# Token transposes by DMA instead of TensorE in a fused cross-attention and maxout kernel

## The chip, the cores and the metric

The kernel runs on one core of a Trainium2 chip. A core has a matrix engine (TensorE, PE in the profile; its weight loads are the row PEld), a vector engine (VectorE, DVE), a scalar engine (ScalarE, ACT), a general engine (GpSimd, POOL) and a sync engine (SyncE, SP) that only issues DMAs. Each engine works off its own queue in order and waits on semaphores for the others. Sixteen DMA engines move the data for all queues. The metric is device time in microseconds for one execution; lower is better.

## The reference

There are 8 batches and 8 heads, each with 512 tokens and 32 state rows of 64 numbers. In every head the tokens read from the state and the state reads from the tokens; then a feed-forward layer with three first matrices, joined by a maximum, follows.

```python
# x: (8, 8, 512, 64), state: (8, 8, 32, 64), float32
scores  = scale * x @ state^T                # tokens look at the state rows
xread   = softmax(scores) @ state            # 512 rows per head
scores2 = scale * state @ x^T                # state rows look at the tokens
sread   = softmax(scores2) @ x               # 32 rows per head
z = concat([xread, sread], axis=2)           # (8, 8, 544, 64)
z = z.transpose(0, 2, 1, 3).reshape(8 * 544, 512)
h = max(z @ w1, z @ w2, z @ w3)              # d_ff = 768
out = h @ w_out                              # (4352, 512), float32
```

## The kernel before

**Layout.** For each batch `x_sb[b]` holds the tokens in bf16 as 128 partitions x 8 heads x 4 x 64: partition p has tokens 4p to 4p+3 of each head. Scores need the 64 numbers of a token on the partitions, so `xt_piece` (L124) makes `xT[b]`: 16 TensorE transposes of 128x128 (two token groups j at a time, 8 heads), all into one PSUM tile `pxt`, which ScalarE copies to SBUF in two halves (L134, L135; in batch 0 VectorE takes the second half). `xT` has two buffers.

**Attention of one batch.** `score_piece` (L137) multiplies `xT` with `bd`, the transposed state blocks, in 16 matmuls into the PSUM tile `ps`; ScalarE takes the exponential into `e` (L146), VectorE the sums `den` (L148) and their reciprocals `rden` (L150), and GpSimd the product `a` (L153; VectorE in batch 0). `e` serves both reads: `sread_piece` (L158) makes the state's read `psr`, which VectorE normalizes into `ats` (L176, L177); `at_piece` (L182) transposes `a` on TensorE into `pat`, which VectorE copies to `aT` (L190).

**Feed-forward.** The state is multiplied into the first matrices beforehand: `g_piece(b, u)` (L195), for u = 0 to 5, makes a sixth of `G[b]` = state x (w1 | w2 | w3), with the PSUM tile `pg` copied by ScalarE (L208). So `x_maxout(b, m)` (L229, with the work in `maxout`, L211) needs only `G` and `aT`: for each of the six column blocks m it fills three PSUM tiles `pw` with two matmuls each (L218), ScalarE copies the first (L222), and VectorE takes the maximum with the second (L223) and the third (L224) into `ht`. `ffn_out(b, j0, j1)` (L239) multiplies two groups of 128 rows of `ht` with `w_out` into `po` in 12 matmuls (L243), ScalarE copies it to `osb` (L251, three buffers), and SyncE stores it (L258).

**Buffers.** PSUM has four buffers of the tag `pw` and two of the tag `two`; `pxt`, `ps`, `psr`, `pat`, `pg` and `po` all take turns in these two. A new tile of the tag waits until the one before it in the same buffer has been copied out.

**Order.** The order of the instructions on every engine is the order of the program: the kernel sets a manual schedule. The main loop over b has six slots m, one after each `x_maxout(b, m)`. In the slots of batch b stands the attention of batch b + 1: `xt_piece` in slot 0, `score_piece` in slot 1, `sread_piece` in slot 3, `at_piece` in slot 4, and `g_piece(b + 1, u)` at the end of each slot u. The output of batch b - 1 stands at the head of slot 2 (first half) and of slot 5 (second half). In the last batch the slots hold the first layer for the state rows (`s_maxout`, L233) in place of the attention.

**Loads.** SyncE loads the tokens of batch 0 in float32. GpSimd's queue converts to bf16 as it loads: six loads of the first matrices, x(1), `w_out`, and from the loop x(b + 2) at the head of batch b (L275). GpSimd also computes `a`, so a load that stands behind an `a` in its queue is issued after it.

Of the kernel before, what the change touches and what calls it, by code (L numbers as in the profile page):

```python
# [15 lines left out]
def kernel(  # L16
# [14 lines left out]
    nc = tc.nc  # L31

    B, H, S, D = x.shape
# [25 lines left out]
    def x_rows(b):  # L59
        return x[b].rearrange("h (p j) d -> p h (j d)", j=J)  # L60

    x_sb = [data.tile([128, H, J, D], BF16, name=f"x{b}") for b in range(B)]
    st_f = data.tile([128, 16, D], F32, name="stf")
    nc.scalar.dma_start(
        out=st_f, in_=state.rearrange("b h n d -> (b h n) d").rearrange("(p t) d -> p t d", t=16))
# [7 lines left out]
    def load_x(b):  # L73
        nc.gpsimd.dma_start(out=x_sb[b].rearrange("p h j d -> p h (j d)"), in_=x_rows(b))
# [4 lines left out]
    def load_w(c):  # L79
        for i, w in enumerate((moe_w1, moe_w2, moe_w3)):  # L80
            nc.gpsimd.dma_start(
                out=w_sb[c][:, :, i * 384:(i + 1) * 384],
                in_=w.rearrange("(kk p) f -> p kk f", p=128)[:, :, c * 384:(c + 1) * 384],
            )

    load_w(0)
    load_w(1)
    load_x(1)
    nc.gpsimd.dma_start(out=wout_sb, in_=moe_w_out.rearrange("(kk p) f -> p kk f", p=128))

    ones = const.tile([128, 64], BF16, name="ones")
# [30 lines left out]
    xT, e, a, aT, G, ht = {}, {}, {}, {}, {}, {}  # L122

    def xt_piece(b):  # L124

        xT[b] = work.tile([128, H, 2, 128], BF16, tag="xT", name="xT")
        pxt = pp.tile([128, H, 2, 128], BF16, tag="two", name="pxt")
        for h in range(H):
            for jj in range(2):
                nc.tensor.transpose(  # L130
                    pxt[:, h, jj, :],
                    x_sb[b][:, h, 2 * jj:2 * jj + 2, :].rearrange("p j d -> p (j d)"), ident)
        second = nc.vector.tensor_copy if b == 0 else nc.scalar.copy
        nc.scalar.copy(out=xT[b][:, 0:4], in_=pxt[:, 0:4])  # L134
        second(out=xT[b][:, 4:8], in_=pxt[:, 4:8])  # L135

    def score_piece(b):  # L137
        ps = pp.tile([128, J, H, Ns], F32, tag="two", name="ps")
        for jj in range(2):
            for h in range(H):  # L140
                nc.tensor.matmul(  # L141
                    ps[:, 2 * jj:2 * jj + 2, slot(h), :], xT[b][:, h, jj, :],
                    bd[:, b, h].rearrange("p c n -> p (c n)"),
                    start=(h == 0), stop=(h == H - 1), skip_group_check=True)
        e[b] = work.tile([128, J, H, Ns], BF16, tag="e", name="e")
        nc.scalar.activation(out=e[b], in_=ps, func=AF.Exp, scale=scale)  # L146
        den = work.tile([128, J, H], F32, tag="den", name="den")
        nc.vector.reduce_sum(out=den, in_=e[b], axis=AX.X)  # L148
        rden = work.tile([128, J, H], F32, tag="rden", name="rden")
        nc.vector.reciprocal(out=rden, in_=den)  # L150
        a[b] = work.tile([128, J, H, Ns], BF16, tag="a", name="a")
        mul = nc.vector.tensor_mul if b == 0 else nc.gpsimd.tensor_mul
        mul(  # L153
            out=a[b].rearrange("p j h n -> p (j h) n"),
            in0=e[b].rearrange("p j h n -> p (j h) n"),
            in1=rden.rearrange("p j h -> p (j h)").unsqueeze(2).to_broadcast((128, J * H, Ns)))
# [38 lines left out]
    def g_piece(b, u):  # L195
        if u == 0:
            G[b] = work.tile([128, 2, 2 * HALF], BF16, tag="G", name="G")
        c, k = divmod(u, 3)
        pg = pp.tile([128, 2, 512], F32, tag="two", name="pg")
        for hh in range(NHP):  # L200
            for r in range(2):
                h = 2 * hh + r
                nc.tensor.matmul(  # L203
                    pg[32 * hh:32 * hh + 32, r, 0:384],
                    bd[64 * r:64 * r + 64, b, h, r, :],
                    w_sb[c][64 * r:64 * r + 64, hh, k * 384:(k + 1) * 384],
                    start=True, stop=True, tile_position=(64 * r, 32 * hh))
        nc.scalar.copy(out=G[b][:, :, u * 384:(u + 1) * 384], in_=pg[:, :, 0:384])  # L208
# [20 lines left out]
    def x_maxout(b, m):  # L229
        maxout(b, m, 512, lambda i, m, k: G[b][:, k, col(i, m):col(i, m) + 128],  # L230
               lambda k: aT[b][:, k, :], 2)

    def s_maxout(m):  # L233
        maxout("s", m, B * Ns,
               lambda i, m, k: w_sb[m // 3][:, k, col(i, m) % HALF:col(i, m) % HALF + 128],
               lambda k: ats[:, k, :], NHP)


    def ffn_out(b, j0, j1):  # L239
        po = pp.tile([128, 2, d_model], F32, tag="two", name="po")  # L240
        for j in range(j0, j1):
            for m in range(NM):
                nc.tensor.matmul(po[:, j - j0, :], ht[b][:, m, j * 128:(j + 1) * 128], wout_sb[:, m, :],  # L243
                                 start=(m == 0), stop=(m == NM - 1))
        n = j1 - j0
        o = work.tile([128, 2, d_model], F32, tag="osb", bufs=3, name="osb")
        if n == 1:
            nc.scalar.copy(out=o[:, 0, 0:256], in_=po[:, 0, 0:256])
            nc.vector.tensor_copy(out=o[:, 0, 256:512], in_=po[:, 0, 256:512])
        else:  # L250
            nc.scalar.copy(out=o, in_=po)  # L251
        if b == "s":
            for k in range(B):
                r0 = k * SP + S
                (nc.sync if k < 4 else nc.gpsimd).dma_start(
                    out=out[r0:r0 + Ns, :], in_=o[32 * (k % 4):32 * (k % 4) + 32, k // 4, :])
            return
        nc.sync.dma_start(  # L258
            out=out[b * SP:b * SP + S, :].rearrange("(p j) f -> p j f", j=J)[:, j0:j1, :],
            in_=o[:, 0:n, :])  # L260


    xt_piece(0)
    score_piece(0)
    bd_piece(1, B)
# [4 lines left out]
    for u in range(3, NG):  # L270
        g_piece(0, u)

    for b in range(B):
        if b + 2 < B:
            load_x(b + 2)  # L275
        slots = [[] for _ in range(NM)]
        if b + 1 < B:
            for f, m in ((xt_piece, 0), (score_piece, 1), (sread_piece, 3), (at_piece, 4)):
                slots[m].append(lambda f=f: f(b + 1))
            for u in range(NG):  # L280
                slots[u].append(lambda u=u: g_piece(b + 1, u))
        else:
            for m in range(NM):
                slots[m].append(lambda m=m: s_maxout(m))
        if b > 0:
            slots[2].insert(0, lambda: ffn_out(b - 1, 0, 2))
            slots[5].insert(0, lambda: ffn_out(b - 1, 2, 4))
        for m in range(NM):
            x_maxout(b, m)
            for f in slots[m]:  # L290
                f()
# [34 lines left out]
```

## Time and profile before

| what | before |
|---|---|
| median of three executions (lowest, highest), us | 190.43 (189.60, 203.50) |
| profiled execution, us | 189.44 |
| its span, first to last instruction, us | 187.6 |
| TensorE busy, us (share of the span) | 163.5 (87%) |
| ScalarE busy | 106.2 (57%) |
| VectorE busy | 103.3 (55%) |
| GpSimd busy | 28.0 (15%) |
| mean granted TensorE clock | 0.996 |
| period of one batch in the steady state, us | 19.04 |

A line of groups gives the source line, the engine, the operation, what it writes and reads, the number of instructions, their busy time with the mean of one in ns, and the idle time of the engine ahead of them with what ended it. A line of the timeline gives the start in us, the duration in us, the engine, the line and the operation, and in square brackets how long the engine was idle before it and what released it. In the rows of tenths, each digit is the busy share of one of 40 slices of the span, 4.7 us each. A DMA line ends with the median time in us from the issue to the landing of the data.

### The profile page before, as it was taken

Reading aid. Unit: us, or ns where it says so; the run is one execution under the profiler, and the core shown is the slowest. Engines: PE = TensorE matmul, PEld = TensorE weight load, DVE = VectorE, ACT = ScalarE, POOL = GpSimd, SP = SyncE. Lnnn points to the kernel's source line nnn. Section 1 sums busy time; section 2 is a strip of 40 time slices with the busy share of each in tenths; the row PEclk is TensorE's granted clock in tenths of the full one; section 3 lists DMA queues with packets and bytes.
Section 4 is the critical chain, followed back from the end, with each engine's and each line's share of the span. In section 5 each row is a group of like instructions: output and inputs, shape, how many; then the busy total and the mean of one; then the engine's idle time right before and its main releaser. Section 6 shows DMA issues by size and latency. Waiting matters only on the chain.

```text
span 187.6 us, 3845 instructions
## 1 busy us (share of the span) xinstructions
PE 163.5 (87%) x1604; PEld 84.8 (45%) x1604; DVE 103.3 (55%) x161; ACT 106.2 (57%) x151; POOL 28.0 (15%) x31
## 2 busy tenths in 40 slices
PE   0643699899999999999999999999999999999990
PEld 0632244454445444544454454445454546565530
DVE  4429325994592559255925683467447747476100
ACT  3542769469455955495549554955495544242330
POOL 8710000500500050005000500040004000000021
PEclk9999999999999999999999999999999999999998
DMA  5999990180192019110911092202020202020236
GB/s 194 265 203 203 203 165 3 6 106 3 77 151 84 31 56 165 68 54 33 182 47 77 9 193 37 103 0 112 5 112 0 115 2 112 3 112 0 112 139 197
DMA packets 15216, 17.53 MB, mean 93 GB/s; under 512 B 672, under 2 KB 12704, under 8 KB 15200
## 3 DMA queue, kind: packets, MB, share of 16 engines
q0 software_dynamic: 11360, 7.08, 27.1%
q1 hardware_dynamic: 3696, 9.70, 13.3%
q10 hardware_dynamic: 144, 0.52, 0.8%
q8 instruction: 12, 0.20, 0.4%
q14 instruction: 4, 0.03, 0.1%
HBM read 15.20 MB, written 8.91 MB: 129 GB/s over the span
## 4 chain that ended last, share of the span: by engine, by line
PE 54%; ACT 18%; DVE 16%; issue 6%; DMA 4%; SPq 0%; DVEq 0%; ACTq 0%
PE pw L218 22%; PE po L243 22%; ACT G L208 7%; PE pg L203 4%; PE pxt L130 4%; DVE rd L176 4%; ACT xT L135 4%; DVE t L223 4%; DMA xf<-in_x_dram 3%; DVE ht L224 3%; ACT xT L134 2%; ACT t L222 2%; ACT osb L251 2%; DVE ats L177 1%; DVE den L148 1%
## 5 line engine op out<-in xcount | busy, mean ns | idle before, releaser
L218 PE MATMUL pw<-aT,G 128*128 128x512 bf16 x288 | 72.0, 384 | 0.7 <-ACT t L222 0.6
L223 DVE TENSOR_TENSOR t<-t,pw 128x512 bf16<-128x512 bf16 (+1 forms) x54 | 34.9, 647 | 55.4 <-ACT t L222 52.1
L208 ACT CAST G<-pg 128x768 bf16<-128x768 f32 x48 | 38.8, 812 | 15.6 <-PE pg L203 15.5
L243 PE MATMUL po<-wout,ht 128*128 128x512 bf16 x204 | 46.5, 379 | 0.0
L218 PEld LDWEIGHTS <-G 128*128 128x128 bf16 x288 | 24.8, 98 | 32.5 <-issue 11.3
L224 DVE TENSOR_TENSOR ht<-t,pw 128x512 bf16<-128x512 bf16 (+1 forms) x54 | 35.5, 658 | 6.0 <-PE pw L218 0.5
L251 ACT COPY osb<-po 128x1024 f32<-128x1024 f32 x16 | 16.2, 1012 | 37.3 <-PE po L243 37.3
L222 ACT CAST t<-pw 128x512 bf16<-128x512 f32 (+1 forms) x54 | 31.4, 584 | 6.9 <-PE pw L218 5.4
L153 POOL TENSOR_TENSOR a<-e,rden 128x1024 bf16<-128x1024 bf16 x7 | 13.3, 1904 | 116.9 <-DVE rden L150 116.9
L243 PEld LDWEIGHTS <-ht 128*128 128x128 bf16 x204 | 19.9, 98 | 23.9
L203 PE MATMUL pg<-w,bd 64*32 64x384 bf16 x384 | 18.1, 353 | 7.2 <-DVE ats L177 6.1
L203 PEld LDWEIGHTS <-bd 64*32 64x32 bf16 x384 | 6.6, 90 | 17.3 <-issue 9.8
L134 ACT COPY xT<-pxt 128x1024 bf16<-128x1024 bf16 x8 | 8.1, 1012 | 5.0 <-PE pxt L130 5.0
L148 DVE TENSOR_REDUCE den<-e 128x32 f32<-128x1024 bf16 x8 | 9.7, 1213 | 2.0 <-ACT e L146 2.0
L130 PE MATMUL pxt<-ident,x 128*128 128x128 bf16 x128 | 9.5, 231 | 0.1
L146 ACT ACTIVATE e<-ps 128x1024 bf16<-128x1024 f32 x8 | 8.5, 1064 | 1.6 <-PE ps L141 1.6
L130 PEld LDWEIGHTS <-x 128*128 128x128 bf16 x128 | 8.5, 104 | 2.0 <-ACT x L109 0.4
L218 PE MATMUL pw<-ats,w 128*128 128x256 bf16 x72 | 9.0, 272 | 0.2 <-ACT t L222 0.2
L141 PE MATMUL ps<-bd,xT 128*128 128x64 bf16 x128 | 5.6, 199 | 3.7 <-ACT xT L135 2.3
L141 PEld LDWEIGHTS <-xT 128*128 128x128 bf16 x128 | 5.1, 101 | 6.9 <-issue 4.3
L218 PEld LDWEIGHTS <-w 128*128 128x128 bf16 x72 | 7.0, 98 | 2.4 <-issue 0.3
L176 DVE RECIPROCAL rd<-psr 128x128 f32<-128x128 f32 x8 | 7.6, 949 | 0.0
(37 smaller groups left out, 78.6 us busy)
## 6 DMA issues: line engine op xcount, KB each, us to landing
out_dram<-osb SPq DMA_DIRECT2D x15, 512.0 KB, 2.6
x<-in_x_dram POOLq DMA_DIRECT2D x7, 512.0 KB, 7.1
w<-in_moe_w_dram POOLq DMA_DIRECT2D x6, 384.0 KB, 10.6
xf<-in_x_dram SPq DMA_DIRECT2D x2, 512.0 KB, 5.9
wout<-in_moe_w_out_dram POOLq DMA_DIRECT2D x1, 768.0 KB, 18.6
stf<-in_state_dram ACTq DMA_DIRECT2D x1, 512.0 KB, 4.1
out_dram<-osb SPq DMA_DIRECT2D x2, 256.0 KB, 3.0
out_dram<-osb SPq DMA_DIRECT2D x4, 64.0 KB, 1.7
```

Source lines behind the costliest of these rows:

```text
L130: nc.tensor.transpose(pxt[:, h, jj, :], x_sb[b][:, h, 2 * jj:2 * jj + 2, :].rearrange("p j d -> p (j d)"), ident)
L134: nc.scalar.copy(out=xT[b][:, 0:4], in_=pxt[:, 0:4])
L153: mul(out=a[b].rearrange("p j h n -> p (j h) n"), in0=e[b].rearrange("p j h n -> p (j h) n"), in1=rden.rearrange("p j h -> p (j h)").unsqu ...
L176: nc.vector.reciprocal(out=rd, in_=psr[:, 128:256])
L203: nc.tensor.matmul(pg[32 * hh:32 * hh + 32, r, 0:384], bd[64 * r:64 * r + 64, b, h, r, :], w_sb[c][64 * r:64 * r + 64, hh, k * 384:(k + 1) ...
L208: nc.scalar.copy(out=G[b][:, :, u * 384:(u + 1) * 384], in_=pg[:, :, 0:384])
L218: nc.tensor.matmul(p[:, 0:n], lhs(i, m, k), rhs(k), start=(k == 0), stop=(k == nk - 1))
L222: nc.scalar.copy(out=t0[:, 0:n], in_=pw[0][:, 0:n])
L223: nc.vector.tensor_max(t1[:, 0:n], t0[:, 0:n], pw[1][:, 0:n])
L224: nc.vector.tensor_max(ht[b][:, m, :], t1[:, 0:n], pw[2][:, 0:n])
L243: nc.tensor.matmul(po[:, j - j0, :], ht[b][:, m, j * 128:(j + 1) * 128], wout_sb[:, m, :], start=(m == 0), stop=(m == NM - 1))
L251: nc.scalar.copy(out=o, in_=po)
```

## The change

The tokens of batches 1 to 7 are transposed by one DMA each, SBUF to SBUF, issued on SyncE. Batch 0 keeps TensorE. The DMA for batch b + 2 is put into slot 3 of batch b; that for batch 1 stands before the loop. Scores move from slot 1 to slot 0, the state's read from slot 3 to slot 2 (behind the output matmuls there). The token loads come one batch earlier: x(2) ahead of `w_out`, and x(b + 3) instead of x(b + 2) in the loop.

```diff
     load_w(1)
     load_x(1)
+    load_x(2)
     nc.gpsimd.dma_start(out=wout_sb, in_=moe_w_out.rearrange("(kk p) f -> p kk f", p=128))
...
         xT[b] = work.tile([128, H, 2, 128], BF16, tag="xT", name="xT")
+        if b > 0:
+            nc.sync.dma_start_transpose(
+                out=xT[b].rearrange("p h j t -> p (h j) t"),
+                in_=x_sb[b].rearrange("p h j d -> p (h j d)"))
+            return
         pxt = pp.tile([128, H, 2, 128], BF16, tag="two", name="pxt")
...
-        second = nc.vector.tensor_copy if b == 0 else nc.scalar.copy
         nc.scalar.copy(out=xT[b][:, 0:4], in_=pxt[:, 0:4])
-        second(out=xT[b][:, 4:8], in_=pxt[:, 4:8])
+        nc.vector.tensor_copy(out=xT[b][:, 4:8], in_=pxt[:, 4:8])
...
+    def xt_next(b):
+        if b + 1 < B:
+            xt_piece(b + 1)
+
...
+    xt_piece(1)
     for b in range(B):
-        if b + 2 < B:
-            load_x(b + 2)
+        if b + 3 < B:
+            load_x(b + 3)
         slots = [[] for _ in range(NM)]
         if b + 1 < B:
-            for f, m in ((xt_piece, 0), (score_piece, 1), (sread_piece, 3), (at_piece, 4)):
+            for f, m in ((score_piece, 0), (sread_piece, 2), (at_piece, 4), (xt_next, 3)):
                 slots[m].append(lambda f=f: f(b + 1))
```

## The prediction

> **What bounds the kernel now.** I read the shares of busy time first, then the tenths per slice, then one batch in order of time on TensorE, ScalarE and VectorE, and last the DMA issues.
>
> ```profile
> PE 163.5 (87%) x1604; PEld 84.8 (45%) x1604; DVE 103.3 (55%) x161; ACT 106.2 (57%) x151; POOL 28.0 (15%) x31
> PE   0643699899999999999999999999999999999990
> DMA  5999990180192019110911092202020202020236
> L130 PE MATMUL pxt<-ident,x 128*128 128x128 bf16 x128 | 9.5, 231 | 0.1
> ```
>
> TensorE is at nine tenths or more from the eighth slice to the last but one: in the steady state it is the bound, and what leaves its queue shortens the batch unless a wait takes its place. The DMA engines are saturated for the first six slices (28 us) and have room later. The token transposes are 128 matmuls, 112 of them concerned.
>
> One batch of before (TensorE, then ScalarE, then VectorE):
>
> ```profile
> 78.69 1.06 PE L130 MATMUL pxt<-ident,x 128*128 128x128 bf16 x16
> 79.68 0.36 PE L203 MATMUL pg<-w,bd 64*32 64x384 bf16 x8
> 79.97 1.47 PE L218 MATMUL pw<-aT,G 128*128 128x512 bf16 x6
> 81.77 0.63 PE L141 MATMUL ps<-bd,xT 128*128 128x64 bf16 x16 [0.33 <-ACT xT L135]
> 91.86 0.36 PE L203 MATMUL pg<-w,bd 64*32 64x384 bf16 x8 [0.33 <-DVE ats L177]
> 97.73 1.06 PE L130 MATMUL pxt<-ident,x 128*128 128x128 bf16 x16
> ...
> 80.69 1.02 ACT L135 COPY xT<-pxt 128x1024 bf16<-128x1024 bf16 x1
> 82.77 1.07 ACT L146 ACTIVATE e<-ps 128x1024 bf16<-128x1024 f32 x1
> ...
> 84.33 1.21 DVE L148 TENSOR_REDUCE den<-e 128x32 f32<-128x1024 bf16 x1
> 85.92 0.63 DVE L223 TENSOR_TENSOR t<-t,pw 128x512 bf16<-128x512 bf16 x1
> ```
>
> The period is 97.73 - 78.69 = 19.04 us. The 16 transposes hold TensorE for 79.68 - 78.69 = 0.99 us (62 ns each; the 231 ns of the page is latency). Scores wait 0.33 us for ScalarE's copies, and one pg waits 0.33 for ats. The exponential and the row sums (den) fall beside the 12 output matmuls, which need neither VectorE nor new pw buffers for 2.7 us.
>
> The DMA issues (size and median time from issue to landing), then the load of batch 1's tokens and their first use by TensorE:
>
> ```profile
> out_dram<-osb SPq DMA_DIRECT2D x15, 512.0 KB, 2.6
> x<-in_x_dram POOLq DMA_DIRECT2D x7, 512.0 KB, 7.1
> out_dram<-osb SPq DMA_DIRECT2D x4, 64.0 KB, 1.7
> 6.18 1.06 POOL L74 DMA_DIRECT2D x<-in_x_dram  x1
> 25.90 1.10 PEld L130 LDWEIGHTS <-x 128*128 128x128 bf16 x16
> ```
>
> The load of x(1) issued at 6.18 lands 15.9 us later (that tile's own landing time), at 22.1; TensorE first reads it at 25.90. So there are 3.8 us of slack between this landing and the use, and in the change a whole DMA transpose has to go into them.
>
> **What the skill says.** Its two prices for the new operation disagree by far. "DMA: Bandwidth & Descriptors", section "Latency and other measured facts", gives 261 GB/s for DMA transposes measured on one kernel. "VectorE: DVE Perf Modes", section "The three transpose paths", gives 1309 ns for one 128x128 bf16 block through the DMA against 390 ns on TensorE. No trace of before has a DMA transpose; TensorE's, back to back, cost 62 ns here. "Advanced Engine Details and Errata", section "DGE: Hardware vs Software", lists the transpose efficiency of the hardware path (SyncE's) as "Worse". And by "DMA: Bandwidth & Descriptors", section "Issuing engines are not separate DMA queues", all queues share the same 16 engines. The trace agrees: the store issued at 68.9, beside an x load issued at 68.98, took 4.3 us to land instead of 2.6.
>
> **The change, part by part.**
>
> *Price of one DMA transpose* (128x2048 bf16, 512 KB, sixteen 128x128 blocks). Low end: 524 kB / 261 GB/s = 2.0 us, plus about 1.6 us of fixed time (the 64 KB store lands after 1.7): 3.6 us. High end: 16 x 1.309 = 21 us. It cannot be below nothing. With nothing to choose between the two I take the geometric middle, 9 us from issue to landing when alone, and keep both ends.
>
> *Removed*: 7 x 16 matmuls with their weight loads (7 x 0.99 us, all on TensorE's path), 14 ScalarE copies of 1.01 us (off the path, ScalarE is at 57%), the wait for xT (0.33).
>
> *Moved*: scores go from slot 1 to slot 0, sread from slot 3 to slot 2, behind the output matmuls. I laid out one batch with the trace's durations and in-order queues (maxout slot 1.30 us, pg 0.29, output 2.68, psr 0.85, pat 0.62, scores 0.70, 0.05 us per wait). Which tile a new PSUM tile waits for, I took from the waits in the compiled order. The old order comes out at 19.03 us, against 19.04 in the trace. The new order, from the first maxout matmul at 0: scores at 1.59, after a 0.29 wait for the last G copy; exponential 2.34 to 3.41; den 3.46, rden 4.74. So VectorE begins slot 1's first maximum only at 5.01, and the third pair of slot 2, which needs that pw buffer, waits 0.71 us, to 5.75. Output matmuls 6.18 to 8.86, psr to 9.71; the copy of po ends at 9.99, so pg waits 0.33. The rest has no wait; the period is 18.41. Check: removed 0.99 + 0.51 (xT wait in my layout) + 0.39 (ats wait) + 0.06, added 0.29 + 0.71 + 0.33: net -0.62 us a batch, not -1.3. The burst of exponential and row sums loses the output matmuls as its cover, and that eats half of the gain. Batch 1 of the loop (my b = 1) gives -0.9.
>
> *Added wait, steady.* The transpose of the next-but-one tokens stands on SyncE behind the store of slot 2: osb copied at 9.99, store issued 0.36 us later, transpose at 10.4. Scores need it at 20.0: 9.6 us of lead. Its own other waits (x landed a batch earlier, xT's buffer free) are over by then. The x load follows `a` on GpSimd, so it is issued at 7.1 and, at 7.1 us to landing, runs until 14.2; that and the store ahead of it on the queue cost the transpose the same 1.7 us that the store at 68.9 lost. 9 + 1.7 = 10.7, landing 21.1, so scores wait 1.1 us: period 19.55, +0.5 against before. This holds for b = 2 to 6: +2.6 us. Behind the waiting scores stands all of TensorE's queue (pg, next maxouts), hence ScalarE and VectorE; behind the transpose on SyncE only the store of slot 5, which has three osb buffers and so costs nothing; without that cover it would cost the transpose's issue time.
>
> *Added wait, start.* The transpose of x(1) starts at 22.1. The other loads run until 28.5 (x(2), issued at 9.57, lands 18.9 us later), so in these 6.4 us it gets half of the engines: 9 + 3.2 = 12.2, landing 34.3. TensorE comes to the scores at 25.3 and stands still for 9 us; ScalarE's backlog and the transposes give 2.3 back: +6.7. The transpose of x(2), behind it, is needed only in the next batch.
>
> *Loads*: x(2) now goes ahead of w_out on GpSimd's queue; w_out then lands near 28.5 instead of 25.8, and is first read at 46.0: nothing. Without that cover it would cost those 2.7 us. Later x loads come a batch earlier than needed: nothing.
>
> *Sum*: +6.7 (b = 0) - 0.9 (b = 1) + 2.6 (b = 2 to 6) = +8.4 us; b = 7 has no such work. The profiled execution took 189.44 us (span 187.6): 197.8, so 198. The median of the runs shown is 190.43, 1.0 above the profiled one.
>
> **The rivals.** *Transposes cheap* (3.6 to 7 us alone): the steady ones hide in 9.6 us, so the batch gets 0.62 shorter (5 x 0.62 + 0.9 = 4.0), and the start decides. At 5.3 us for the first (3.6 + 1.7) the layout gives -4.2, 185.3; at 8.5, -1.0, 188.5; even at 9.5. It ends not slower as long as the first lands within 9.5 us of its issue and the later ones within 9.6. For it: 261 GB/s, DMA engines at two tenths in most steady slices. Against: the saturated start and "Worse". *Transposes by the block* (13 to 21 us): the period becomes issue-to-landing plus 8.8 us, the transpose is then the bound; at 21 us (24 and 22.6 with contention) it is +80, 269 (each us of price adds one in the start and one in each of five batches); at 13 (16.2 and 14.7) +32, 222. For it: 1309 ns; against: sixteen blocks should overlap. *No effect of the move*: TensorE's compiled queue has 224 rows fewer, 7 x 32, so the transposes do leave it; I give that nothing.
>
> **The numbers.** A price spread evenly on a log scale from 3.6 to 21 us has 0.38 under 7 (cheap), 0.35 from 7 to 13 (190 to 222, with the forecast) and 0.27 above. By the same sum, faster by over 2% needs a price under some 4.5 us: 0.12; within 2% goes up to some 8.3: 0.33; slower: 0.55. Two per cent is about what a measurement of this kernel tells from no change. Range: 185.5 (lowest price) to 235, a price of 15 us, beyond which 0.18 is left, with 0.02 below.
>
> **What would show it.** Scores in the after trace wait for the DMA: about 9 us in the first batch, 1 us in the later ones; transposes land 9 to 12 us from issue; between scores and output matmuls a pw matmul waits some 0.7 us for VectorE; psr is followed by a 0.3 us wait for osb. The forecast is wrong if the transposes land within 7 us (then 185 to 189), or if each takes over 13 us and scores wait in every batch for longer than the batch gains.

## The result and the profile after

| what | before | after |
|---|---|---|
| median, us (same chip) | 190.30 | 192.75 |
| ratio, 95% interval | | 1.0136 [1.0094, 1.0177] |
| profiled execution, us | 189.44 | 192.83 |
| its span, us | 187.6 | 191.0 |
| batch b = 0 of the loop, us | 15.28 | 23.04 |
| batch b = 1, us | 19.03 | 17.91 |
| each of b = 2 to 6, us | 19.04 | 18.39 |

The changed kernel is slower by 1.4%, within the 2% of "no change" and inside the range, but by far less than the forecast of 198 us. One of the four executions of before was a slow one, 203.5 us; it counts in the median of 190.30 and is left out of the ratio. The profiled execution of before, at 189.44 us, lies under its median, so the profiles differ by 3.4 us and the medians by about 2.5. The batch times are the distances between the first maxout matmuls of two batches, read from the timelines. The record of the very first one is missing in the changed kernel; the five after it come 0.43 us apart from 24.50 on, so it began at about 24.07, and b = 0 is counted from there. The batches account for the difference of the spans: the loop begins about 0.03 us later, b = 0 costs 7.76 us more, b = 1 gives 1.12 back and b = 2 to 6 give 3.27: +3.4 us, of 191.0 - 187.6 = 3.4.

The page of the changed kernel: busy time, and the tenths of TensorE and of the DMA engines in 40 slices of 4.8 us.

```profile
PE 156.1 (82%) x1468; PEld 77.9 (41%) x1492; DVE 104.6 (55%) x161; ACT 94.2 (49%) x137; POOL 28.3 (15%) x31
PE   0742650799999989998999899989998999999990
DMA  6999999617049226920894044205320202020236
```

With the 112 transposes and their 14 copies gone, TensorE is busy for 7 us less and ScalarE for 12. But the sixth and seventh slices of TensorE (24 to 33 us), in which the loop begins, now read 5 and 0 instead of 9 and 9. That hole lies where the DMA engines are still saturated.

The timeline of TensorE after: the start of the loop, then one batch of the steady state.

```profile
24.50 2.34 PE L223 MATMUL pw<-aT,G 128*128 128x512 bf16 x5 [0.34 <-issue]
34.84 1.04 PE L146 MATMUL ps<-bd,xT 128*128 128x64 bf16 x16 [8.01 <-DMA xT<-x]
36.26 2.58 PE L223 MATMUL pw<-aT,G 128*128 128x512 bf16 x6
39.06 1.47 PE L223 MATMUL pw<-aT,G 128*128 128x512 bf16 x6
...
84.71 0.63 PE L146 MATMUL ps<-bd,xT 128*128 128x64 bf16 x16
89.12 0.59 PE L223 MATMUL pw<-aT,G 128*128 128x512 bf16 x2 [0.83 <-DVE t L228]
93.40 0.36 PE L208 MATMUL pg<-w,bd 64*32 64x384 bf16 x8 [0.25 <-ACT osb L256]
103.09 0.63 PE L146 MATMUL ps<-bd,xT 128*128 128x64 bf16 x16
```

The scores of batch 1 wait 8 us for the DMA transpose, and the work on both sides of that wait runs slowly: the pw matmuls ahead of it and behind it come 0.43 us apart, later 0.22 (six take 2.58 us, later 1.47). In the steady state the scores wait for nothing. In their place stand the two new waits of the walk through the batch: 0.83 us for VectorE and 0.25 us for the copy of po.

The DMA view after, whole run: packets, and the transposes with their median time from issue to landing.

```profile
DMA packets 29775, 21.19 MB, mean 111 GB/s; under 512 B 15232, under 2 KB 27264, under 8 KB 29760
xT<-x SPq DMA_TRANSPOSE x7, 7.7
```

Before, 672 packets were under 512 bytes. The 14,560 more are 2,080 for each of the seven transposes, some 252 bytes each on average (524 kB / 2,080): 2,048 of 256 bytes and 32 of 4. The first transpose took 12.2 us to land, those of the steady state 4.9 to 8.1.

### The profile page after: what moved, and what is told of

It is laid out like the page before. It is cut to its first block, busy times and chain, and to the rows that moved or that the text cites. A ratio compares the mean times of both kernels' runs of the same rounds, so it can differ in the third digit from the quotient of the medians.

```text
span 191.0 us, 3590 instructions
## 1 busy us (share of the span) xinstructions
PE 156.1 (82%) x1468; PEld 77.9 (41%) x1492; DVE 104.6 (55%) x161; ACT 94.2 (49%) x137; POOL 28.3 (15%) x31
## 4 chain that ended last, share of the span: by engine, by line
PE 54%; DMA 15%; DVE 11%; ACT 9%; issue 5%; POOL 3%; DVEq 0%; POOLq 0%; ACTq 0%
PE pw L223 25%; PE po L248 23%; DMA x<-in_x_dram 8%; DMA xT<-x 6%; DVE t L228 5%; ACT osb L256 4%; PE pg L208 4%; DVE den L153 4%; POOL w L81 3%; ACT G L213 3%; DVE ht L229 3%; ACT t L227 2%; PE pat L191 2%; PE ps L146 1%; ACT e L151 1%
## 5 line engine op out<-in xcount | busy, mean ns | idle before, releaser
L248 PE MATMUL po<-wout,ht 128*128 128x512 bf16 x196 | 46.0, 379 | 0.4
L213 ACT CAST G<-pg 128x768 bf16<-128x768 f32 x48 | 38.3, 803 | 15.4 <-PE pg L208 15.2
L227 ACT CAST t<-pw 128x512 bf16<-128x512 f32 (+1 forms) x54 | 30.9, 574 | 6.9 <-PE pw L223 5.4
L153 DVE TENSOR_REDUCE den<-e 128x32 f32<-128x1024 bf16 x8 | 9.7, 1215 | 11.5 <-ACT e L151 11.4
L208 PEld LDWEIGHTS <-bd 64*32 64x32 bf16 x384 | 5.9, 90 | 18.9 <-issue 12.6
L146 PEld LDWEIGHTS <-xT 128*128 128x128 bf16 x128 | 5.4, 106 | 12.2 <-DMA xT<-x 8.9
L260 POOL DMA_DIRECT2D out_dram<-osb x4 | 2.1, 525 | 39.3 <-ACT osb L256 39.3
L195 DVE COPY aT<-pat 128x1024 bf16<-128x1024 bf16 x8 | 5.5, 685 | 2.5 <-PE pat L191 2.5
L168 PEld LDWEIGHTS <-x 128*64 128x64 bf16 x256 | 5.1, 118 | 4.1 <-issue 4.0
```

The source lines that it names most:

```text
L146: nc.tensor.matmul(ps[:, 2 * jj:2 * jj + 2, slot(h), :], xT[b][:, h, jj, :], bd[:, b, h].rearrange("p c n -> p (c n)"), start=(h == 0), st ...
L208: nc.tensor.matmul(pg[32 * hh:32 * hh + 32, r, 0:384], bd[64 * r:64 * r + 64, b, h, r, :], w_sb[c][64 * r:64 * r + 64, hh, k * 384:(k + 1) ...
L227: nc.scalar.copy(out=t0[:, 0:n], in_=pw[0][:, 0:n])
```

## The experiments

After the result the theory was: one wait, in the start, costs all that the change loses; it is long because of the loads beside it; in the steady state the DMA is free, and the moved slots take back half of what it frees. The rivals: transposes that are slow by themselves, or a steady cost that the start hides.

**Batch 1 on TensorE.**

```diff
-        if b > 0:
+        if b > 1:
             nc.sync.dma_start_transpose(
```

> Batch 1's tokens are transposed by TensorE ahead of the loop; batches 2 to 7 keep the DMA and the new slots. Theory (the whole loss is the one wait for batch 1's transpose in the saturated start, the steady state gains 0.66 us a batch): no score waits for a DMA, loop batch 0 takes about 14 us instead of 22.6, the steady period stays 18.4, the time is about 185.5, ratio to before 0.975. Rival (the DMA transposes cost something in every batch that the start hides): the time stays above 189.

Measured: 186.01 us, ratio 0.974 [0.9707, 0.9773], span 184.3; no score waits for a DMA, and the period is 18.38 us (scores at 77.75, 96.13, 114.52). The steady state is faster than before, and the one wait turned the gain into a loss.

**Nothing loaded beside the first transpose.**

```diff
-    load_x(2)
-    nc.gpsimd.dma_start(out=wout_sb, ...)
...
     xt_piece(1)
+    hold = const.tile([128, 1], BF16, name="hold")
+    nc.gpsimd.tensor_copy(out=hold, in_=xT[1][:, 0, 0, 0:1])
+    load_x(2)
+    nc.gpsimd.dma_start(out=wout_sb, ...)
```

> All seven transposes by DMA, but the loads of x(2), w_out and x(3) are issued only after batch 1's transpose has landed (one small GpSimd copy that reads it stands ahead of them). Theory (the first transpose took 12.2 us because of the loads beside it): it lands in 5 to 6 us, its scores wait 2 us or less, the time is about 186.5, ratio 0.98. Rival (a transpose costs about 9 us by itself, or the first one is slow for its own reasons): it still takes 9 us or more, scores wait over 5 us and the time is 190 or more.

Measured: 193.55 us, ratio 1.0131 [1.0096, 1.0167]. The time was missed, the reason for it was not. The DMA view of this kernel from 22.5 to 26.5 us, with the first transpose alone, and then the timeline at the scores of batch 2:

```profile
q1 hardware_dynamic: 2080, 0.52, 68.9%
xT<-x SPq DMA_TRANSPOSE x1, 4.3
```

```profile
46.93 1.04 PE L144 MATMUL ps<-bd,xT 128*128 128x64 bf16 x16 [6.25 <-DMA xT<-x]
```

Alone, a transpose lands in 4.3 us. Its 2,080 packets took 68.9% of 16 engines for 4 us, 21 ns each. But x(2), held back, landed only at 33.1; the transpose of batch 2 then ran beside w_out, x(3) and x(4), whose last landed at 47.1, and took 13.7 us, to 46.9. The wait had moved from batch 1 to batch 2. I had not worked out that next transpose.

**x(3) out of the start.**

```diff
-        if b + 3 < B:
-            load_x(b + 3)
+        if 0 < b and b + 2 < B:
+            load_x(b + 2)
```

> The changed kernel, but x(3) and the later loads are issued one batch later, as in the kernel before, so that x(3) is not loaded in the start. Theory (a transpose's 256-byte packets take turns with the load's packets one by one, so it is slow for as long as any load runs, and x(3) makes the loads run some 3 us longer): the first transpose lands in about 9 us instead of 12.2, its scores wait about 5 us instead of 8, time about 189.5. Rival (the transpose gets half of the engines' time and x(3) stands behind it anyway): it still lands in 12 us, time 192.5.

Measured: 189.60 us, ratio 0.9965 [0.9946, 0.9984]; the first transpose lands after 8.8 us.

```profile
31.50 1.03 PE L146 MATMUL ps<-bd,xT 128*128 128x64 bf16 x16 [3.36 <-DMA xT<-x]
```

The last load of the start (w_out) lands at 29.7 here and the transpose at 31.5. In the changed kernel x(3), issued at 11.5, lands at 34.1, and the transpose at 34.8. In both, the transpose comes through soon after the last load. The edit issues the later loads a batch later as well, but the period stays at 18.39 us, so the gain lies in the start. Moving x(3) forward, which looked free, cost 3 us by the ratios (1.0136 and 0.9965), more than the whole loss: without it the change is level with before.

**The old slots.**

```diff
-            for f, m in ((score_piece, 0), (sread_piece, 2), (at_piece, 4), (xt_next, 3)):
+            for f, m in ((score_piece, 1), (sread_piece, 3), (at_piece, 4), (xt_next, 3)):
```

> All seven transposes by DMA, but scores back in slot 1 and the state's read in slot 3, as before. Theory (the new slots put the exponential and the row sums on two maxouts without the output matmuls as cover, worth some 0.6 us a batch): steady period 17.8 us, the 0.8 us wait of a pw matmul for VectorE is gone, the 0.33 us wait for ats is back; the first wait for the DMA is about 6.5 us and the time about 188.5, ratio 0.99. Rival (the slots don't matter, the gain is bounded elsewhere): period 18.4, time about 191.5.

Measured: 188.16 us, ratio 0.9836 [0.9794, 0.9879], first wait 4.79 us, where 6.5 was expected. The timeline of TensorE in its steady state:

```profile
101.23 0.63 PE L146 MATMUL ps<-bd,xT 128*128 128x64 bf16 x16
111.14 0.36 PE L208 MATMUL pg<-w,bd 64*32 64x384 bf16 x8 [0.33 <-DVE ats L182]
118.93 0.63 PE L146 MATMUL ps<-bd,xT 128*128 128x64 bf16 x16
```

The period is 17.70 us: 19.04 - 17.70 = 1.34 is the 0.99 of the transposes, the 0.33 of the wait for xT and hardly anything else. The pw matmuls wait no more, the wait for ats is back. So the moved slots cost 18.39 - 17.70 = 0.69 us a batch.

**The new slots without the DMA.**

```diff
-        if b > 0:
+        if b > B:
             nc.sync.dma_start_transpose(
...
-        nc.vector.tensor_copy(out=xT[b][:, 4:8], in_=pxt[:, 4:8])
+        second = nc.vector.tensor_copy if b == 0 else nc.scalar.copy
+        second(out=xT[b][:, 4:8], in_=pxt[:, 4:8])
```

> The new slots and the earlier loads, with TensorE's transposes and ScalarE's copies where the DMAs stood (slot 3 for the batch after next, batch 1 ahead of the loop). Theory (a DMA transpose in the steady state takes exactly its TensorE time off and costs nothing): period 18.4 + 1.0 = 19.4 us, time about 191 to 192, ratio 1.005. Rival (the DMA transposes slow the steady state by contention): period under 19.2, time under 190.

Measured: 196.58 us, ratio 1.0292 [1.0252, 1.0332]; period 19.98 us, more than I expected.

```profile
83.59 0.63 PE L147 MATMUL ps<-bd,xT 128*128 128x64 bf16 x16
96.95 0.61 PE L192 MATMUL pat<-ident,a 128*128 128x128 bf16 x8 [0.33 <-ACT xT L141]
103.57 0.63 PE L147 MATMUL ps<-bd,xT 128*128 128x64 bf16 x16
```

Beside the 0.99 us for the transposes, their copies on ScalarE come in the way at this place: `pat` waits for them (0.33), and small gaps make up the rest. With these slots the DMA saves 19.98 - 18.39 = 1.6 us a batch. Nothing here speaks for a steady cost of the DMA transposes.

**One more transpose.**

```diff
+        if b > 2:
+            xdup = work.tile([128, H, 2, 128], BF16, tag="xdup", name="xdup")
+            nc.sync.dma_start_transpose(out=xdup..., in_=x_sb[b]...)
```

> The changed kernel with one more DMA transpose, into a buffer that nobody reads, ahead of each of batches 3 to 7. Theory (a transpose has 9.6 us from its issue until the scores need it, and uses 5 to 8 of them): the needed one now lands 10 to 13 us after the pair's issue, scores wait 1.5 to 3 us while x loads run beside it and little in the last two batches; period 20 to 21 us for batches with an x load, time about 199 to 203, ratio 1.04 to 1.06. Rival (the steady transposes have far more room than that): period stays 18.4 and the time 193.

Measured: 193.96 us, ratio 1.0179 [1.0134, 1.0225]; most batches stay at 18.4 us. I had added a contended transpose to a contended one, but when the first is through, the x load is over, and the second needs only 4.3 to 6.0 us. One batch is late. SyncE's queue there, then TensorE's timeline:

```profile
94.70 5.55 SPq L130 DMA_TRANSPOSE xdup<-x  x1
100.34 1.89 SPq L134 DMA_TRANSPOSE xT<-x  x1
```

```profile
104.73 0.64 PE L151 MATMUL ps<-bd,xT 128*128 128x64 bf16 x16 [0.58 <-ACT t L232]
```

The needed one lands 4.3 us after its issue, at 104.69, so the pair took 10.0 us and the scores waited 0.58 us. (The line names ScalarE's t, as the last event it can see; the landing at 104.69 fits the start at 104.73.) A room of 9.4 us from issue to scores, then: the 9.6 of the prediction is right, and the transposes of the change, at 4.9 to 8.1 us, fit.

**Both losses removed.** Batch 1 on TensorE and the old slots, the two edits above together.

> Batch 1 on TensorE ahead of the loop, batches 2 to 7 by DMA, scores in slot 1 and the state's read in slot 3. Theory (two separate losses in the change, the wait in the start and the moved slots): no wait for a DMA, steady period 17.7 us as in the run with the old slots, time about 181, ratio to before 0.95. Rival (with the first wait gone another wait, for example for batch 2's transpose, takes its place): a score wait of some us in the second batch and a time above 185.

Measured: 182.47 us, ratio 0.9581 [0.9539, 0.9623], period 17.70 us, no score waits for a DMA. The time is 1.5 us above the expected 181, but the period is the one expected, and no other wait took the place of the first.

**x(1) loaded earlier, all seven by DMA, old slots.**

```diff
     load_w(0)
-    load_w(1)
     load_x(1)
+    load_w(1)
```

> All seven transposes by DMA, old slots, and the load of x(1) ahead of the second half of the first matrices. Theory (what matters is when x(1) lands, since a transpose needs about 12 us beside saturating loads): the first transpose starts near 15 us and lands before 29, no score waits for it, but the second half of the first matrices lands some 2 us later and may hold one or two pg; time 181 to 183.5, ratio 0.95 to 0.965. Rival (a transpose so early only delays the weights by as much as it saved): 186 or more.

Measured: 183.22 us, ratio 0.9628 [0.9577, 0.9679]. The first transpose is issued at 15.9 but takes 15.7 us, since loads now run beside it all the time (x(3) lands at 36.7, after it); it lands at 31.6 and the scores wait 2.60 us. The wait was not gone, as I had expected, but the time came out in the range.

**The DMA for batches 2 to 7 alone.** Slots, loads and batch 1 are those of before.

```diff
+        if b > 1:
+            nc.sync.dma_start_transpose(...)
+            return
...
-            for f, m in ((xt_piece, 0), (score_piece, 1), (sread_piece, 3), (at_piece, 4)):
+            for f, m in ((score_piece, 1), (sread_piece, 3), (at_piece, 4), (xt_next, 3)):
+        if b == 0:
+            slots[0].append(lambda: xt_piece(1))
```

> The kernel before with one thing changed: batches 2 to 7 transposed by DMA, issued in slot 3 of the batch before their use. Slots, loads and batch 1 (TensorE, slot 0) are as before. Theory (the gain is the TensorE time of the transposes and the wait for their copies, 1.35 us a batch; earlier loads and moved slots gave nothing): period 17.7 us, time 182 to 183, ratio 0.955 to 0.96. Rival (the earlier loads are needed for the transposes to land in time): scores wait for the DMA in the later batches, time 185 or more.

Measured: 182.51 us, ratio 0.9551 [0.9513, 0.9589]; scores at 60.05, 77.75, 95.45, a period of 17.70.

```profile
77.75 0.63 PE L146 MATMUL ps<-bd,xT 128*128 128x64 bf16 x16
95.45 0.63 PE L146 MATMUL ps<-bd,xT 128*128 128x64 bf16 x16
```

The transposes take 9.7 us in the median here, beside the later x loads, and are still in time, since scores in slot 1 leave them more room: 11.2 us from the issue at 66.54 to the scores at 77.75. It is just enough: the slowest, of 11.0 us, lands 0.2 us before its scores. So neither the earlier loads nor the new slots are needed. The last three versions beat both kernels, and their intervals overlap.

**The wait filled.** Twenty-eight matmuls into a pw tile that nobody reads stand ahead of batch 1's scores.

```diff
+        if b == 0:
+            def fill():
+                p = pp.tile([128, 512], F32, tag="pw", bufs=4, name="fill")
+                for _ in range(28):
+                    nc.tensor.matmul(p, w_sb[0][:, 0, 0:128], w_sb[0][:, 0, 0:512], start=True, stop=True)
+            slots[0].append(fill)
```

> The changed kernel with 28 matmuls that nobody reads ahead of batch 1's scores, so that TensorE works while it would wait for the first DMA transpose. Theory (after the 8 us wait TensorE runs at half speed for some 3 us more, so the wait costs its own length and about 1.7 us beside): the scores and the six pw matmuls after the wait take 0.6 and 1.5 us instead of 1.0 and 2.6, the time falls by 1 to 1.7 us against the changed kernel, to about 191.3. Rival (those matmuls are slow for another reason, their operands come late): no change, 192.8, or later by the filling work.

> The changed kernel itself beside the filled one, so that a difference of 1 us is read on the same chip: 192.8, ratio 1.013; first transpose 12 us from issue to landing, scores of batch 1 waiting 8 us, period 18.4.

Measured on the same chip: 191.59 us filled, ratio 1.0051 [1.003, 1.0072], and 192.83 unfilled, 1.0108 [1.0074, 1.0142]. The timeline of the filled one, then of the unfilled one:

```profile
27.36 6.21 PE L291 MATMUL fill<-w 128*128 128x512 bf16 x28
34.53 0.64 PE L146 MATMUL ps<-bd,xT 128*128 128x64 bf16 x16 [0.96 <-DMA xT<-x]
35.39 1.47 PE L223 MATMUL pw<-aT,G 128*128 128x512 bf16 x6
```

```profile
24.60 2.74 PE L223 MATMUL pw<-aT,G 128*128 128x512 bf16 x6
34.84 1.03 PE L146 MATMUL ps<-bd,xT 128*128 128x64 bf16 x16 [7.50 <-DMA xT<-x]
36.26 2.71 PE L223 MATMUL pw<-aT,G 128*128 128x512 bf16 x6
```

The transpose lands in 12.2 us in both. (TensorE comes to its wait half a microsecond later here than in the first profile of the changed kernel, hence 7.50 and not 8.01.) From the scores of batch 1 to those of batch 2 it is 12.41 us filled and 13.71 unfilled. So work that is of no use made the kernel 1.2 us faster: without it TensorE runs at half of its speed after the wait. It did not fall to that speed in this wait, for the six pw matmuls ahead of it take as long (2.74 us): the wait began before TensorE had come up. In the kernel before, it comes up within the first six and works on:

```profile
24.04 2.24 PE L218 MATMUL pw<-aT,G 128*128 128x512 bf16 x6
27.39 1.47 PE L218 MATMUL pw<-aT,G 128*128 128x512 bf16 x6
```

A fall is seen in the run with the old slots. There the pw matmuls ahead of the wait are at full speed and those behind it are not, and the granted clock reads 0.50 from 35.3 to 38.6 us:

```profile
28.44 1.47 PE L223 MATMUL pw<-aT,G 128*128 128x512 bf16 x6
34.70 0.64 PE L146 MATMUL ps<-bd,xT 128*128 128x64 bf16 x16 [4.79 <-DMA xT<-x]
35.73 2.74 PE L223 MATMUL pw<-aT,G 128*128 128x512 bf16 x6
```

The page "TensorE: Matmul & The Clock Gate" of the Trainium skill, section "Part 1: The HAM clock gate", describes both: half speed is where the clock starts and where an idle window of about 3.4 us puts it, and full speed comes after as long a time of work. The trace agrees: the stretch at half speed in the run with the old slots lasts 3.4 us. In the changed kernel the row of the granted clock shows nothing of it, since the trace has no record of the clock before 38.6 us and the row prints time without a record as full; the durations do show it.

## Why the prediction was wrong

**The step that failed is the price of one DMA transpose.** It took the geometric middle, 9 us, of 3.6 and 21 us. Alone it is 4.3 us (the quiet start), 0.7 above the low end. The 261 GB/s of the skill's "Latency and other measured facts" came near (alone, the 524 kB moved in 2.6 us, some 200 GB/s); 1309 ns for a single block, multiplied by sixteen, did not. In "Added wait, steady" this made 10.7 us against a room of 9.6, where 4.9 to 8.1 were measured: instead of +0.5 us a batch the change gave -0.65, and over five batches -3.3 instead of +2.6. (The 1.7 us for what runs beside it was read from one store, the one at 68.9; the three other stores that before issues beside an x load took 2.7 to 3.2 us.) That is 5.9 us; the sum was too high by 5.0 (+8.4 against +3.4), since the start came out 1.1 us dearer and b = 1 0.2 us cheaper than forecast.

**The start came out right for the wrong reasons.** The forecast was 12.2 us to the landing and so it was, but as 9 + 3.2, "half of the engines" until 28.5. With the true price the same reasoning gives about 7: 2.7 us of packets at half speed, and 1.6 of fixed time. Two things were missed. First, from 22.6, where the transpose is issued, to 26.5 us only the loads move in the changed kernel:

```profile
q0 software_dynamic: 976, 0.80, 129.8%
```

The first packet of the transpose comes 3.9 us after its issue, against 1.2 with nothing beside it in the quiet start. Why it comes so late beside loads stays open. Second, a transpose that has begun does not get half of what it would move alone. From 27 to 31 us:

```profile
q0 software_dynamic: 897, 0.49, 87.3%
q1 hardware_dynamic: 902, 0.23, 45.5%
```

The queues take turns packet for packet, 902 of the transpose and 897 of the loads, and as evenly in each microsecond (234 and 234 from 28 to 29). (The shares add up to more than 100%, so packets overlap in time.) But the load's packets are larger, so the transpose gets a third of the bytes and of the time: 226 packets a us, where alone it moves its 2,080 in 2.6 us, 800 a us. The skill's "DMA: Bandwidth & Descriptors", section "Queues, rings and completion order", says that an engine alternates between queues by packets; these counts agree. So the landing moves with the loads: 4.3 us without any, 8.8 where the last lands at 29.7, 12.2 where it lands at 34.1, and 15.7 where loads run all the time.

And "Loads: later x loads come a batch earlier than needed: nothing" was wrong: the load of x(3) moved into the start and made it 3 us longer. A third thing was missed as well, TensorE's half speed after the wait, 1.2 us. With the scores' wait of 8.0 instead of 9, the start came to +7.8 against the +6.7 forecast.

**Smaller slips.** TensorE's eighth slice reads 8, not 9. In the batch of before only the row sums fall beside the output matmuls (84.11 to 86.86); the exponential ends at 83.84. And with 4.5 and 8.3 us as the bounds, the chances come out at 0.13, 0.35 and 0.53. None of these changes the forecast.

**What held.** The walk through a batch: 18.41 us forecast, 18.39 measured; the wait for VectorE 0.71 and 0.83, for osb 0.33 and 0.25, no wait for ats, b = 1 -0.9 and -1.1. The loss of the cover of the output matmuls, 0.69 us a batch by the run with the old slots. The room of 9.6 us (9.4). w_out, landing at 29.7 now and first read at 52.8, cost nothing by itself, and nobody waited behind the transposes on SyncE. The rival that came true is "transposes cheap", "the start decides"; its own limit, a first landing within 9.5 us, is where the run without x(3) ended level (8.8 us, 0.9965).

## What to carry to other kernels

A DMA that is cheap in the middle of a kernel can be the longest wait in its start, where loads hold all engines: work out the first use separately, count every load that the change moves in front of it or beside it, and leave the first piece on a compute engine if there is no room. When work leaves the bound engine, keep the old slots first: moving the consumer earlier took half of the gain here by taking the cover from a burst on another engine. And a wait of several microseconds on TensorE can cost more than its length: here 1.2 us beside the 8.

## What the runs showed of the hardware that was not expected

- A DMA transpose of 512 KB (128x2048 bf16, SBUF to SBUF) on SyncE lands 4.3 us after its issue with nothing beside it, 4.3 to 11.4 in the steady state of these kernels, beside a store or an x load or neither, and 8.8 to 15.7 where loads of the start run beside it and it is the first.
- Beside a load on another queue its 256-byte packets go one for one with the load's (902 and 897 in 4 us), at 226 a us instead of 800.
- It holds SyncE itself for 1.9 to 7.6 us, longest beside loads, where a store's issue takes 0.33. Nothing here waited for that; what an urgent DMA behind a transpose would lose was not tried.
- TensorE's 512-column matmuls came 0.43 us apart instead of 0.22 on both sides of an 8 us wait, for some 4 us behind it, with the row of the granted clock at full.
